# Four tiles instead of two in the product with w_out1, z in six half-pair places, and a new opening list

## The chip, the cores and the metric

The kernel runs on one NeuronCore of a Trainium2 chip. What counts is the device time of one execution in microseconds (us), and lower is better. Five engines work side by side, each through its own instructions in order: TensorE (PE, matrix products; its weight loads are listed as PEld), VectorE (DVE), ScalarE (ACT), GpSimd (POOL) and SyncE (SP), which here only issues DMAs. An engine waits on semaphores of the others.

## The reference, cut to what matters

```python
# attention in chunks of 64 keys: 8 batches, 8 heads, 576 tokens, head size 64
scores = scale * q_c @ k_c.T;  attn = softmax(scores);  out = attn @ v_c
x = out.transpose(0, 2, 1, 3).reshape(4608, 512)
# first layer, 512 -> 1024 -> 512
h = x @ w_in1
solu = h * softmax(h)
z = (solu - mean(solu)) / sqrt(var(solu) + 1e-6)
y = (z * g_ln) @ w_out1
# second layer, 512 -> 2048 -> 512
h = y @ w_in2
out = (max(h, 0) + alpha * min(h, 0)) @ w_out2
```

Inputs of the layers are 64-bit floats in DRAM. Their words are turned into float32 on the chip.

## The kernel before, in words

The 4608 tokens are 36 tiles of 128. **The first part** runs them through attention, the first layer's two products and the normalisation between. Beside that it converts all weights: a unit is one 128x512 piece of a weight matrix; units 0 to 7 are w_in1, 8 to 15 w_out1, 16 to 47 the second layer's, which are also split into a high and a low half and written back to DRAM. **The second part** computes the second layer with a scheme of seven products in place of eight, for the rows w_in2 first and w_out2 after it.

Each float32 product is three products of halves (function `mm3`): high by high, high by low, low by high. The halves of x are `xh` and `xl`, those of z `zh` and `zl`, those of the weights `wi_h`, `wi_l`, `wo_h`, `wo_l`.

The steps of a tile i in the order of its data have short names, which the lists use:

- attention: `q`, `v` loads; `qk` scores (PE, 32 products); `qm` maximum and difference (DVE), `qe` exponential (ACT), `qs` sum and reciprocal (DVE), `qn` scaling (POOL for the first twelve tiles, then DVE); `tr` transposition (PE), `te` its copy (ACT), `pv` product with v (PE); `xh` (ACT) and `xl` (DVE) the halves of x.
- first layer: `hm` x by w_in1 (PE, 24 products of 512 columns), `hx` maximum (DVE), `he` exponential (ACT), `so` product of h and softmax (DVE), `sq` squares (ACT), `zv`, `pw`, `zs` variance and scaling (DVE, POOL, DVE), `zt` transposition (PE, 8), `zh` (ACT) and `zl` (DVE) its halves; `ya`, `yb` two blocks of z by w_out1 (PE), `ye` copy of the result from PSUM (ACT) and its store to DRAM.
- weights, unit u: `f` load, `p` two sign parts (ACT, two instructions), `s` or `S` their difference (POOL or DVE), `l` low word (DVE, two instructions), `a` or `A` sum (POOL or DVE), `h` high half (ACT), `o` or `O` low half (POOL or DVE).

The order is written by hand. `FIRST` is the list of all steps up to tile 10, `STEP` the steps of one iteration i of the loop over the other tiles (`ya-5` is the step `ya` of number i-5), `CONV` the weight steps inside it, `LAST` the end of the first part, in which `sy` are steps of the second part. Every engine takes its own instructions in this order.

Before, a group of the product with w_out1 is two tiles (YT = 2, 256 columns), and its 512 output rows are four blocks of 128 rows. Step number s computes two of the blocks for the group s // 2, in `ya` and `yb`: 24 products of 256 columns each (8 pieces of the inner size 1024 times 3 halves). z has three buffers of two tiles, zh and zl apart. The first group can start once tile 1 is through. In the opening the words of w_in1 (`rawt`) lie in these z buffers, and so do the halves of x of tiles 2 to 5 (`xt`). The result goes from PSUM with one ACT copy for two blocks and a DMA on ACT's queue. `ps_a` has three PSUM banks, which `sc` (scores), `et` (transposed) and `xd` (attention output) take in turn; the result of `hm` has two banks, that of `zt` two, that of `ya` and `yb` one.

At the start of the second part the weights `w` of its eight blocks are loaded on SP's queue: the first two into room left by x, the next ones into room that z, w_out1 and the result of the product leave.

Of the kernel before, what the change touches and what calls it, by code (L numbers as in the profile page):

```python
# [42 lines left out]
def order(text):  # L43
# [12 lines left out]
    xl4 p9 te5 a8 qk7 qn6 pv5 hx0 he0 qm7 f11 s9 q9 p10 tr6 so0 l9 qe7 qs7 v8 qk8 s10 sq0 zv0 hm1
    xh5 pw0 h8 q10 qk9 qm8 a9 l10 p11 zs0 v6 te6 xl5 o8 qe8 a10 h9 hx1 he1 qs8 zt0 so1 f12 qm9 zh0
    qn7 tr7 p12 zl0 sq1 f13 s11 q11 s12 pv6 q12 zv1 h10 f14 qe9 l11 hm2 p13 pw1 v9 zs1 te7 f15 a11
    qs9 hx2 qn8 h11 l12 zt1 he2 o10 pv7 xh6 tr8 so2 xl6 p14 hm3 al0 S14 a12 qn9 te8 zh1 o11 zl1 xh7
    o9 qk10 sq2 zv2 l14 tr9 pw2 zs2 xl7 S13 zt2 p15 hx3 l13 h12 a14 he3 s15 so3 f16 te9 zh2 pv8 zl2  # L60
    pv9 h14 hm4 qm10 a13 h13 f18 f17 v12 o12 O13 p16 o14 sq3 l15 zv3 qe10 A15 pw3 zs3 f20 p18 v10
    f19 qs10 s16 zt3 h15 o15 l16 v11 hx4 s18 he4 p17 so4 A16 sq4 f21 s17 ya0 yb0 zv4 hm5 p20 ye0 zh3
    l17 ya1 yb1 pw4 l18 hm6 hx5 f22 he5 p19 qn10 a17 ye1 zs4 zl3 so5 a18 p21 xh8 sq5 S19 zv5 zt4 pw5
    h18 zs5 ya2 yb2 zh4 hx6 he6 h17 o18 zt5 zl4 l19 zh5 so6 o17 sq6 zv6 pw6 zl5 hm7 s20 zs6 zt6 ye2
    h16 hx7 he7 so7 xh9 xl8 zh6 sq7 ya3 yb3 zv7 S21 l20 pw7 zs7 hm8 tr10 zl6 hx8 zt7 qk11 a19 te10
    pv10 xl9 he8 f23 so8 sq8 zh7 hm9 qm11 zv8 ye3 zl7 xh10 hx9 ya4 yb4 pw8 qe11 zs8 he9 so9 sq9 h19
    zv9 qs11 qn11 A20 pw9 xl10 zs9 zt8 o16
# [5 lines left out]
    ya-5 conv+1 xh+1 xl+1 zv+0 pw+0 qs+2 zs+0 qn+2 yb-5  # L73
# [16 lines left out]
def tile_chunk_attention_solu_prelu(  # L90
# [74 lines left out]
    def phase1():  # L165
        with ExitStack() as c1, ExitStack() as c0:
# [11 lines left out]
            ztp = R("zt", YL // 2)  # L178
# [21 lines left out]
            wo_h = wop.tile([128, KF1, DM], F32R, name="wo_h")  # L200
            wo_l = wop.tile([128, KF1, DM], F32R, name="wo_l")
# [6 lines left out]
            for kk in range(KF1):  # L208
                units.append((w_out1[kk * 128:(kk + 1) * 128, :], wo_h[:, kk], wo_l[:, kk]))
# [89 lines left out]
            def run_post(k):  # L299
# [14 lines left out]
            xt = [ztp.tile([128, 2, 2, NP, 128], F32R, name=f"xe{k}", tag=t) for k, t in enumerate(("zh", "zl"))]  # L314
# [92 lines left out]
            def pv(i):  # L407
# [3 lines left out]
                ps = ps_a.tile([128, NP, 2, CH], F32, name="xd", tag="a")  # L411
# [80 lines left out]
            def zscale(i):  # L492
                st, s = ss.pop((i, 5))
                nc.vector.tensor_scalar(
                    out=s, in0=s, scalar1=st[:, 4:5], scalar2=st[:, 7:8], op0=ALU.add, op1=ALU.mult
                )
                zz[i] = s

            ztt, zps = {}, {}

            def ztr(i):
                z = zz.pop(i)
                ps = ps_z.tile([128, KF1, 128], F32, name="zt", tag="zt")
# [23 lines left out]
            ypools = [ps_y]  # L527

            def ymm(s, m):
                j, half = divmod(s, 2)  # L530
                assert ("zl", 2 * j + 1) in done and all(("o", u) in done for u in range(UI, UO))
                zh, zl = ztt[j]
                if m == 0:
                    ypend[s] = ypools[(s + 1) % len(ypools)].tile([128, 2, YG], F32, name="yps", tag="yps")
                else:
                    assert ("ya", s) in done
                ps = ypend[s][:, m]
                c = slice((2 * half + m) * 128, (2 * half + m + 1) * 128)
                for kk in range(KF1):
                    mm3(ps, wo_h[:, kk, c], wo_l[:, kk, c], zh[:, kk], zl[:, kk], kk == 0, kk == KF1 - 1)  # L540
                if half and m:
                    del ztt[j]

            def yevac(s):
                assert ("yb", s) in done
                j, half = divmod(s, 2)
                y = yp.tile([128, 2, YG], F32, name="ysb", tag="ysb")
                nc.scalar.activation(out=y, in_=ypend.pop(s), func=AF.Copy)  # L548
                g, o = divmod(j * YG, 2 * SG)
                nc.scalar.dma_start(out=y_dram[g][:, 2 * half:2 * half + 2, o:o + YG], in_=y)  # L550
# [13 lines left out]
                zt=ztr, zh=zhigh, zl=zlow, ya=lambda s: ymm(s, 0), yb=lambda s: ymm(s, 1), ye=yevac,  # L564
# [4 lines left out]
                {k: TILES for k in "q v qk qm qe qs qn tr te pv xh xl hm hx he so sq zv pw zs zt zh zl ya yb ye".split()},  # L569
# [43 lines left out]
            with tc.tile_pool(name="ps_y2", bufs=1, side="left", space=PSUM, reuse_waits="tile") as ps_y2:  # L613
                ypools.append(ps_y2)
                for name, i in LAST:
                    if name == "sy":
                        next(second)
                    else:
                        emit(name, i)
# [477 lines left out]
```

## Time and profile before

| | us |
|---|---|
| median of three runs | 1294.31 (1292.63 to 1296.69) |
| the profiled execution | 1296.48 |
| its span in the trace | 1294.1 |
| PE busy in the span | 1246.7 (96%) |
| DVE, ACT, POOL busy | 947.8, 686.5, 328.2 |
| products with w_out1, of 128x256 | 3 x 576 |

The trace gives times from the span's start. Matmuls are pipelined and their listed durations overlap; the pace of a stream is read from start to start. The granted clock of TensorE (PEclk) is given as a share of its full speed. The stretches of the opening are cut where `hx0`, `hm5` and `hm10` begin.

### The profile page before, as it was taken

How to read it: one execution, taken by the hardware profiler on the slowest of the kernel's cores; microseconds unless marked ns; L12 is line 12 of the kernel's file. 1: busy time of each engine (PE TensorE's matmuls, PEld its weight loads, DVE VectorE, ACT ScalarE, POOL GpSimd, SP SyncE). 2: the span in 40 equal slices, each digit the busy share in tenths (PEclk: the TensorE clock that was granted, in tenths of full speed). 3: DMA queues.
4: the chain of work that ended last, by engine and by line, in shares of the span. 5: the costliest groups of instructions: out<-in, count | busy, mean ns of one | idle time of the engine just before them, and what ended most of it. 6: DMA issues, size and time to landing. Idle time of an engine off the chain costs nothing.

```text
span 1294.1 us, 23429 instructions
## 1 busy us (share of the span) xinstructions
PE 1246.7 (96%) x9024; PEld 1152.0 (89%) x9024; DVE 947.8 (73%) x1423; ACT 686.5 (53%) x1140; POOL 328.2 (25%) x309
## 2 busy tenths in 40 slices
PE   4789899999999989999999999999999999999998
PEld 4678789999889989899999999999999788888898
DVE  6996677777878766535878787877876959768684
ACT  5685355555556555434757575766634434444443
POOL 4563245343657464332020202020000000000000
PEclk8799999999999999999999999999999999999999
DMA  8443246564656463269642434436996647375462
GB/s 304 161 132 108 80 149 187 162 188 154 201 192 221 155 212 106 75 244 339 225 153 110 159 111 159 149 121 247 365 344 192 236 138 266 120 246 172 147 227 98
DMA packets 144655, 237.99 MB, mean 184 GB/s; under 512 B 13856, under 2 KB 99360, under 8 KB 142496
## 3 DMA queue, kind: packets, MB, share of 16 engines
q1 hardware_dynamic: 134592, 226.27, 51.1%
q10 hardware_dynamic: 9792, 9.44, 2.1%
q8 instruction: 71, 1.16, 0.4%
q0 software_dynamic: 160, 0.79, 0.1%
q14 instruction: 40, 0.33, 0.1%
HBM read 149.68 MB, written 86.77 MB: 183 GB/s over the span
## 4 chain that ended last, share of the span: by engine, by line
PE 48%; DMA 2%; DVE 1%; ACT 0%; issue 0%; DVEq 0%; ACTq 0%; SPq 0%
PE oz L955 7%; PE ov L955 7%; PE hz L722 7%; PE ox L955 7%; PE hx L722 7%; PE hv L722 7%; PE oy L955 3%; PE hy L722 3%; DMA gd<-g 2%; DMA rc<-gd 1%; DVE rt L636 0%; DVE rb L636 0%; DVE rlo L636 0%; ACT rhi L639 0%; ACT g L639 0%
## 5 line engine op out<-in xcount | busy, mean ns | idle before, releaser
L161 PE MATMUL yps<-zh,wo_h 128*128 128x256 f32 x576 | 165.4, 287 | 0.7 <-ACT ysb L548 0.7
L163 PE MATMUL yps<-zh,wo_l 128*128 128x256 f32 x576 | 163.0, 283 | 0.0
L162 PE MATMUL yps<-zl,wo_h 128*128 128x256 f32 x576 | 162.9, 283 | 0.0
L761 DVE SCALAR_TENSOR_TENSOR g<-ng,nal,g 128x384 f32<-128x384 f32 x192 | 124.7, 649 | 50.4 <-ACT g L639 50.3
L639 ACT ACTIVATE ng<-g 128x384 f32<-128x384 f32 x144 | 75.8, 526 | 117.2 <-DVE g L633 117.2
L722 PE MATMUL hv<-th,w 128*128 128x384 f32 x384 | 113.0, 334 | 0.3 <-DVE g L633 0.3
L722 PE MATMUL hz<-th,w 128*128 128x384 f32 x384 | 113.1, 335 | 0.2 <-DVE wv L633 0.2
L722 PE MATMUL hx<-th,w 128*128 128x384 f32 x384 | 113.0, 334 | 0.0
L161 PEld LDWEIGHTS yps<-zh,wo_h 128*128 128x128 f32 x576 | 110.5, 192 | 1.0 <-ACT ysb L548 0.9
L162 PEld LDWEIGHTS yps<-zl,wo_h 128*128 128x128 f32 x576 | 110.4, 192 | 0.1
L163 PEld LDWEIGHTS yps<-zh,wo_l 128*128 128x128 f32 x576 | 110.3, 192 | 0.0
L955 PE MATMUL oz<-rhi,w 128*128 128x512 f32 (+1 forms) x304 | 93.8, 369 | 0.8 <-DVE osb L633 0.8
L955 PE MATMUL ox<-rhi,w 128*128 128x512 f32 (+1 forms) x304 | 93.7, 369 | 0.0
L955 PE MATMUL ov<-rhi,w 128*128 128x512 f32 (+1 forms) x304 | 93.7, 369 | 0.0
L636 POOL TENSOR_TENSOR yt<-y,y 128x384 f32<-128x384 f32 x24 | 27.1, 1152 | 234.2 <-DMA y<-yd 136.8
L639 ACT ACTIVATE rhi<-rt 128x1024 fp32r<-128x1024 f32 (+1 forms) x56 | 54.5, 984 | 59.5 <-DVE rt L636 16.3
L443 PE MATMUL h<-wi_h,xh 128*128 128x512 f32 x256 | 71.0, 399 | 6.5 <-DVE sl L471 4.6
L639 ACT ACTIVATE g<-g 128x384 f32<-128x384 f32 x144 | 75.2, 522 | 3.1
L523 DVE TENSOR_TENSOR zl<-zt,zh 128x1024 fp32r<-128x1024 f32 x36 | 44.0, 1221 | 43.5 <-ACT zh L518 43.5
L636 DVE TENSOR_TENSOR rlo<-rt,rhi 128x1024 fp32r<-128x1024 f32 (+1 forms) x56 | 62.3, 1125 | 13.8 <-ACT rhi L639 13.7
L722 PEld LDWEIGHTS hz<-th,w 128*128 128x128 f32 x384 | 70.7, 188 | 0.7 <-DVE wv L633 0.7
L722 PEld LDWEIGHTS hv<-th,w 128*128 128x128 f32 x384 | 70.7, 188 | 0.6 <-DVE g L633 0.6
(176 smaller groups left out, 3320.6 us busy)
## 6 DMA issues: line engine op xcount, KB each, us to landing
gd<-g SPq DMA_DIRECT2D x192, 192.0 KB, 1.8
qkt<-in_qk SPq DMA_DIRECT2D x36, 512.0 KB, 5.7
w<-wid SPq DMA_DIRECT2D x8, 1792.0 KB, 9.6
w<-wod SPq DMA_DIRECT2D x8, 1792.0 KB, 9.6
rc<-gd SPq DMA_DIRECT2D x24, 512.0 KB, 4.3
rd<-gd SPq DMA_DIRECT2D x24, 512.0 KB, 5.1
raw<-in_moe_w_out SPq DMA_DIRECT2D x24, 511.8 KB, 4.2
vt<-in_v SPq DMA_DIRECT2D x36, 256.0 KB, 5.2
```

The source lines that it names most:

```text
L161: nc.tensor.matmul(o, lh, rh, start=first, stop=False)
L162: nc.tensor.matmul(o, lh, rl, start=False, stop=False)
L163: nc.tensor.matmul(o, ll, rh, start=False, stop=last)
L443: nc.tensor.matmul(ps[:, n], xh[:, kk], w[:, kk, 512 * n:512 * n + 512], start=(kk == 0 and w is wi_h), stop=False,)
L523: nc.vector.tensor_tensor(out=zl, in0=ps, in1=zh.bitcast(F32), op=ALU.subtract)
L636: eng.tensor_tensor(out=out, in0=a, in1=b, op=ALU.subtract)
L639: nc.scalar.activation(out=out, in_=in_, func=func, **k)
L722: nc.tensor.matmul(self.ps[x], w[:, a, i, k], d[:, k], start=(p not in CHAINED and k + j == 0), stop=(k == 1 and j == 2), skip_group_check ...
L761: nc.vector.scalar_tensor_tensor(out=self.g[t], in0=self.n[t], scalar=nal_sb[:, f:f + 1], in1=self.g[t], op0=ALU.mult, op1=ALU.add)
L955: nc.tensor.matmul(bank[key, m][:, :n], W[2 * j + k][:, a, i, 128 * m:128 * m + 128], d[:, k], start=(p not in CHAINED and j + k + q == 0) ...
```

## The change

The product takes groups of four tiles (YT = 4): 512 columns in one matmul, 12 products in a `ya` and 12 in a `yb`. z lies in one tile `zz` of six places. A place holds both halves of half of the inner size (4 of 8 pieces) for a pair of tiles (256 columns); a table `Z_SLOTS` says which two places a pair takes. The matmul's moving operand is thus two runs of 256 columns, from two places. In a group, steps 0 and 1 compute a block each, and steps 2 and 3 together two blocks, the first half of the inner size for both in step 2 (`ya`, `yb`), the second half in step 3. A group's first pair of places is free for new z after step 2, the second after step 3.

`ye` stores one block of 512 columns, not two of 256, by two DMAs on SP's queue; a new step `yx` does so for the block that is complete after `ya` of step 3. PSUM: the result has two banks, `sc` and `et` one each, and `xd` shares et's bank (in the first eight tiles that of the result). w_in1's words lie in the room of `wo_h` and `wo_l`, which are made when unit 8 is converted. `FIRST` is a new order; `STEP` gets `yx-5` at its end; `LAST` is adapted, without the additional PSUM pool.

```diff
-YT = 2
+YT = 4
 YG = 128 * YT
-YL = 6
+YP = 256
...
 STEP = order(
     """
     q+3 v+3 ye-6 zh-2 zl-2 conv+0 hm+0 tr+1 te+1 qk+2 hx+0 he+0 qm+2 qe+2 pv+1 zt-1 so+0 sq+0
-    ya-5 conv+1 xh+1 xl+1 zv+0 pw+0 qs+2 zs+0 qn+2 yb-5
+    ya-5 conv+1 xh+1 xl+1 zv+0 pw+0 qs+2 zs+0 qn+2 yb-5 yx-5
...
-    zh34 zl34 ye30 ya31 yb31 zt35 zh35 zl35 ye31 ya32 yb32 sy0 sy1 ye32 ya33 yb33 sy2 sy3
-    ye33 ya34 yb34 sy4 sy5 ye34 ya35 yb35 sy6 sy7 ye35
+    zh34 zl34 ye30 ya31 zt35 yb31 zh35 zl35 yx31 ye31 ya32 yb32 sy0 sy1 ye32 ya33 yb33 sy2 sy3
+    ye33 ya34 yb34 sy4 sy5 ya35 yb35 sy6 yx35 sy7 ye35
...
+Z_SLOTS = (
+    ((0, 1), (2, 4)), ((3, 5), (0, 2)), ((1, 4), (0, 3)), ((2, 5), (0, 1)), ((3, 4), (0, 2)),
+    ((1, 5), (0, 3)), ((2, 4), (0, 1)), ((3, 5), (0, 2)), ((1, 4), (0, 3)),
+)
...
-            ps_a = L("ps_a", 3, space=PSUM)
+            ps_a = L("ps_a", 1, space=PSUM)
...
-            ps_y = R("ps_y", 1, space=PSUM)
+            ps_y = R("ps_y", 2, space=PSUM)
...
+            zz = ztp.tile([128, 6, 2, KF1 // 2, YP], F32R, name="zz")
             rawt = [
-                ztp.tile([128, 2, 512, 4], U16, name=f"wraw{kk}", tag="zh" if kk % 2 == 0 else "zl")
-                for kk in range(K1)
+                r[:, k] for t in ("h", "l")
+                for r in [wop.tile([128, 2, 2, 512, 4], U16, name=f"wraw{t}", tag=f"wo_{t}")] for k in range(2)
             ]
...
+            def yblock(j, m, h):
+                a, b = sorted(x[h] for x in Z_SLOTS[j])
+                if h == 0:
+                    ypend[j, m] = ps_y.tile([128, YG], F32, name="yps", tag="yps")
+                ps = ypend[j, m]
+                zh, zl = (zz[:, a:b + 1:b - a, n] for n in range(2))
+                c = slice(m * 128, m * 128 + 128)
+                for k in range(KF1 // 2):
+                    kk = KF1 // 2 * h + k
+                    mm3(ps, wo["h"][:, kk, c], wo["l"][:, kk, c], zh[:, :, k], zl[:, :, k], kk == 0, kk == KF1 - 1)
+
+            def ymm(s, n):
+                j, q = divmod(s, YT)
+                assert ("zl", YT * j + 3) in done and all(("o", u) in done for u in range(UI, UO))
+                assert n == 0 or ("ya", s) in done
+                if q < 2:
+                    yblock(j, q, n)
                 else:
+                    yblock(j, 2 + n, q - 2)
+
+            def ystore(j, m):
+                y = yp.tile([128, YG], F32, name="ysb", tag="ysb")
+                nc.scalar.activation(out=y, in_=ypend.pop((j, m)), func=AF.Copy)
+                pairs = (0, 1) if Z_SLOTS[j][0][0] < Z_SLOTS[j][1][0] else (1, 0)
+                for c, p in enumerate(pairs):
+                    g, o = divmod(j * YG + p * YP, 2 * SG)
+                    nc.sync.dma_start(out=y_dram[g][:, m, o:o + YP], in_=y[:, c * YP:(c + 1) * YP])
```

The opening list is new as a whole. It moves steps on every engine; three places are shown.

**ACT at the very start.** `pos` and `neg` are step `p` of a unit, `e` is `qe0`, `ets` is `te0`. Before:

```order
L555 ACTIVATE mhalf<-mhalf 128x1
L139 ACTIVATE pos<-wraw_133,b_64 128x512
L140 ACTIVATE neg<-wraw_133,b_64 128x512
L139 ACTIVATE pos<-wraw_133,b_64 128x512
L140 ACTIVATE neg<-wraw_133,b_64 128x512
L381 ACTIVATE e<-e 128x512
L139 ACTIVATE pos<-wraw_134,b_64 128x512
```

Now, at the same place:

```order
L585 ACTIVATE mhalf<-mhalf 128x1
L142 ACTIVATE pos<-wrawh,b_64 128x512
L143 ACTIVATE neg<-wrawh,b_64 128x512
L391 ACTIVATE e<-e 128x512
L142 ACTIVATE pos<-wrawh,b_64 128x512
L143 ACTIVATE neg<-wrawh,b_64 128x512
L414 ACTIVATE ets<-et 128x512
```

The first exponential now stands behind one unit's `p` and not behind two.

**PE in the opening, around its first product with w_out1.** `zt` is the transposition of z of tile 3 in both, `h` is `hm`. Before, `hm4` ends here, `zt3` follows, then the first `ya`:

```order
L443 MATMUL h<-wi_h,xe_138 128x512 x4
L443 MATMUL h<-wi_l,xe_138 128x512 x4
L449 MATMUL h<-wi_h,xe_138 128x512 x8
L505 MATMUL zt<-ident,sl 128x128 x8
L161 MATMUL yps<-zh,wo_h 128x256
L162 MATMUL yps<-zl,wo_h 128x256
L163 MATMUL yps<-zh,wo_l 128x256
```

Now `hm5` stands between the transposition and the first `ya` (which is number 1), and each product has 512 columns:

```order
L518 MATMUL zt<-ident,sl 128x128 x8
L456 MATMUL h<-wi_h,zz 128x512 x4
L456 MATMUL h<-wi_l,zz 128x512 x4
L456 MATMUL h<-wi_h,zz 128x512 x4
L456 MATMUL h<-wi_l,zz 128x512 x4
L462 MATMUL h<-wi_h,zz 128x512 x8
L164 MATMUL yps<-zz,wo_h 128x512
L165 MATMUL yps<-zz,wo_h 128x512
L166 MATMUL yps<-zz,wo_l 128x512
```

`ya0` and `yb0`, which stood ahead of `hm5`, now come after it and after `ya1`, `yb1` and `hm6`.

**SP at the start of the second part.** `w20` to `w24` are the weights of its blocks 0 to 4, `y11` to `y21` its first inputs, `yd` the first part's result in DRAM. Before (the stores of that result are on ACT's queue):

```order
L684 DMA y21_6848<-yd0_65 128x2x384
L658 DMA w20_6850<-wid_71 128x3584
L658 DMA w21_6852<-wid_71 128x3584
L658 DMA w22_7209<-wid_71 128x3584
L658 DMA w23_7211<-wid_71 128x3584
L658 DMA w24_7233<-wid_71 128x3584
```

Now:

```order
L712 DMA y21_6098<-yd0_65 128x2x384
L686 DMA w20_6100<-wid_71 128x3584
L686 DMA w21_6102<-wid_71 128x3584
L569 DMA yd5_70<-ysb_6141 128x256
L569 DMA yd4_69<-ysb_6141 128x256
L569 DMA yd5_70<-ysb_6145 128x256
L569 DMA yd4_69<-ysb_6145 128x256
L569 DMA yd5_70<-ysb_6188 128x256 x2
L569 DMA yd5_70<-ysb_6225 128x256 x2
L569 DMA yd5_70<-ysb_6289 128x256 x2
L569 DMA yd5_70<-ysb_6297 128x256 x2
L686 DMA w22_6338<-wid_71 128x3584
```

Twelve stores of the first part stand between `w21` and `w22`.

## Rows read from the trace of the kernel before

**Rows 1.** The page's first part: busy time, share, instructions of each engine

```profile
PE 1246.7 (96%) x9024; PEld 1152.0 (89%) x9024; DVE 947.8 (73%) x1423; ACT 686.5 (53%) x1140; POOL 328.2 (25%) x309
```

**Rows 2.** Stretches of the opening: window, length, busy us per engine, PEclk, DMA share

```profile
10.80:45.15 34.35, 22.33 (x373) 19.72 (x373) 31.79 (x53) 20.31 (x35) 18.59 (x16) 0.75 0.75 270
...
55.75:109.25 53.50, 46.35 (x485) 38.99 (x483) 47.98 (x85) 41.31 (x67) 30.65 (x27) 0.97 0.46 147
109.25:173.07 63.82, 59.57 (x420) 53.41 (x421) 37.71 (x63) 28.87 (x46) 17.91 (x17) 0.97 0.24 75
173.07:533.73 360.66, 355.78 (x3556) 324.27 (x3554) 268.15 (x444) 198.22 (x321) 186.94 (x173) 1.00 0.54 176
```

**Rows 3.** One iteration of the loop, PE: start us, us, instruction, count

```profile
271.21 0.36 PE L161 MATMUL yps<-zh,wo_h 128*128 128x256 f32 x1
271.41 0.28 PE L162 MATMUL yps<-zl,wo_h 128*128 128x256 f32 x1
...
277.05 1.09 PE L443 MATMUL h<-wi_h,xh 128*128 128x512 f32 x4
...
282.52 0.60 PE L399 MATMUL et<-ident,e 128*128 128x128 f32 x4
...
285.91 0.36 PE L161 MATMUL yps<-zh,wo_h 128*128 128x256 f32 x1
```

**Rows 4.** Stretches of the second part, one product form each: 384, 512 columns

```profile
700.00:750.00 50.00, 50.00 (x290) 50.00 (x289) 38.83 (x68) 31.49 (x68) 9.44 (x8) 1.00 0.40 143
...
1100.00:1150.00 50.00, 50.00 (x223) 41.40 (x222) 32.72 (x31) 21.43 (x22) 0.00 (x0) 1.00 0.45 149
```

**Rows 5.** The opening, PE, in order of time

```profile
102.42 0.36 PE L161 MATMUL yps<-zh,wo_h 128*128 128x256 f32 x1
...
109.25 1.17 PE L443 MATMUL h<-wi_h,xe 128*128 128x512 f32 x4 [0.84 <-DVE sl L471]
...
137.12 2.06 PE L443 MATMUL h<-wi_h,xh 128*128 128x512 f32 x4 [3.23 <-DVE sl L471]
138.97 1.83 PE L443 MATMUL h<-wi_l,xh 128*128 128x512 f32 x4
140.64 1.09 PE L443 MATMUL h<-wi_h,xh 128*128 128x512 f32 x4
...
160.91 1.21 PE L443 MATMUL h<-wi_h,xh 128*128 128x512 f32 x4 [1.03 <-DVE sl L471]
```

**Rows 6.** The first steps, ACT

```profile
7.59 0.73 ACT L140 ACTIVATE neg<-wraw,b 128x512 uint16<-128x512 uint16 x1
...
10.16 0.61 ACT L381 ACTIVATE e<-e 128x512 f32<-128x512 f32 x1
```

**Rows 7.** DVE ahead of hm5: step qs10, then hx4 and so4

```profile
101.37 0.67 DVE L385 TENSOR_REDUCE r<-e 128x8 f32<-128x512 f32 x1
...
103.20 1.08 DVE L151 TENSOR_SCALAR g<-a 128x512 uint16<-128x512 uint16 x1
...
104.93 1.22 DVE L457 TENSOR_REDUCE st<-h 128x1 f32<-128x1024 f32 x1
...
107.81 1.28 DVE L471 SCALAR_TENSOR_TENSOR sl<-h,st,eh 128x1024 f32<-128x1024 f32 x1
```

**Rows 8.** An iteration of the loop on DVE, ACT and SP

```profile
289.29 0.69 DVE L434 TENSOR_TENSOR xl<-xd,xh 128x512 fp32r<-128x512 f32 x1 [1.85 <-ACT xh L429]
...
291.95 0.60 ACT L548 ACTIVATE ysb<-yps 128x512 f32<-128x512 f32 x1 [2.69 <-PE yps L163]
...
294.56 0.38 SPq L232 DMA_DIRECT2D wid<-hi  x1
```

**Rows 9.** Loads of the second part's weights, SP, and their landing; its first product

```profile
579.55 0.80 SPq L658 DMA_DIRECT2D w<-wid  x2
...
DMA to landing us min/median/max: 8.2/9.2/13.3
...
590.95 0.34 PE L722 MATMUL hx<-th,w 128*128 128x384 f32 x1
```

More of the change, by code (lines that the diff above doesn't have):

```diff
@@ L56 @@
[L56 to L65, printed above, removed]
@@ L66 @@
-    pv10 xl9 he8 f23 so8 sq8 zh7 hm9 qm11 zv8 ye3 zl7 xh10 hx9 ya4 yb4 pw8 qe11 zs8 he9 so9 sq9 h19
-    zv9 qs11 qn11 A20 pw9 xl10 zs9 zt8 o16
+    q0 f0 p0 q1 qk0 f1 q8 qk1 qm0 f3 qe0 q9 f2 p1 qs0 s0 qn0 tr0 te0 l0 v0 a0 q2 pv0 q12 qm1 f5 p3 q7 S1
+    qe1 qk2 l1 q3 A1 f4 v1 qs1 p2 S2 h1 qm2 xh0 q4 v2 l2 h0 p5 qe2 s3 xl0 v4 qk3 qn1 o0 qs2 O1 a2 f8 p4
+    qm3 qn2 l3 tr1 v7 f7 f6 te1 h2 tr2 q5 qe3 pv1 a3 S4 v3 f10 xh1 qs3 qk4 o2 qn3 te2 p7 qm4 qe4 pv2 S5
+    l4 h16 tr3 l5 A4 xh2 q6 qs4 te3 a5 p6 s7 xl2 f9 xl1 qk5 qm5 p8 h4 v8 v5 h5 qn4 h3 s6 O4 tr4 f11 qe5
@@ new lines @@
+    l13 xl6 f21 a13 te8 h12 f17 zt2 he3 zh2 f19 p16 f20 tr9 so3 h13 zl2 sq3 qm10 hm4 s15 pv8 qk11 te9
+    l15 s16 xh7 zv3 h14 A15 p18 pw3 s18 o16 O13 o14 l16 h15 o9 hx4 o12 he4 zs3 o15 zt3 so4 sq4 zh3 l18
+    zv4 qe10 p17 zl3 A16 hm5 s17 hx5 ya1 he5 l17 yb1 so5 sq5 ye1 hm6 p19 a17 ya0 qs10 zv5 pw4 h18 xl7
+    zs4 xh8 pw5 f22 hx6 zt4 zh4 he6 yb0 zs5 a18 zt5 zl4 h19 ya2 xl8 hm7 p20 so6 S19 zh5 s20 ye0 v9 sq6
+    zl5 zv6 pw6 pv9 zs6 hx7 he7 so7 p21 sq7 zt6 yb2 zh6 hm8 v12 v10 xh9 h17 zv7 xl9 l19 o18 hx8 pw7 zl6
@@ L68 @@
+    qn10 tr10 a19 zs7 qm11 o17 te10 he8 ya3 yb3 zt7 so8 pv10 sq8 zh7 zl7 hm9 l20 f23 ya4 zv8 hx9 S21 ye3
+    he9 pw8 ye2 yx3 xh10 A20 zs8 so9 sq9 qe11 zv9 qs11 pw9 xl10 qn11 zs9 yb4 zt8
     """
@@ L208, in phase1 @@
             for kk in range(KF1):
-                units.append((w_out1[kk * 128:(kk + 1) * 128, :], wo_h[:, kk], wo_l[:, kk]))
+                units.append((w_out1[kk * 128:(kk + 1) * 128, :], None, None))
             UI, UO = 2 * K1, 2 * K1 + KF1
@@ L345, in unit_hi @@
                 else:
-                    his[u] = units[u][1]
+                    if u == UI:
+                        assert all(("l", x) in done for x in range(UI))
+                        for t in "hl":
+                            wo[t] = wop.tile([128, KF1, DM], F32R, name=f"wo_{t}", tag=f"wo_{t}")
+                    his[u] = wo["h"][:, u - UI]
                     nc.scalar.activation(out=f, in_=f, func=AF.Copy, scale=g_sb[:, u - UI:u - UI + 1])
@@ L396, in tr @@
                 e = ee.pop((i, 1)).rearrange("q (j w) k -> q j (w k)", w=2)
-                ps = ps_a.tile([128, NP, 128], F32, name="et", tag="a")
+                ps = ps_a.tile([128, NP, 128], F32, name="et", tag="et")
                 for p in range(NP):
@@ L410, in pv @@
                 v = vs.pop(i)
-                ps = ps_a.tile([128, NP, 2, CH], F32, name="xd", tag="a")
+                if i < 8:
+                    ps = ps_y.tile([128, NP, 2, CH], F32, name="xd", tag="yps")
+                else:
+                    ps = ps_a.tile([128, NP, 2, CH], F32, name="xd", tag="et")
                 for c in range(2):
@@ L526, in phase1 @@
             ypend = {}
[L527 to L534, printed above, removed]
-                else:
[L536 to L542, printed above, removed]
+            def yblock(j, m, h):
[8 more added lines that the diff above has]
+                    mm3(ps, wo["h"][:, kk, c], wo["l"][:, kk, c], zh[:, :, k], zl[:, :, k], kk == 0, kk == KF1 - 1)
@@ L544, in yevac, with yfirst @@
             def yevac(s):
                 assert ("yb", s) in done
[L546 to L550, printed above, removed]
+                j, q = divmod(s, YT)
+                if q != 2:
+                    ystore(j, q)
+            def yfirst(s):
+                j, q = divmod(s, YT)
+                if q == 3:
+                    ystore(j, 2)
@@ L612, in phase1 @@
             next(second)
[L613 to L619, printed above, removed]
+            for name, i in LAST:
+                if name == "sy":
+                    next(second)
+                else:
+                    emit(name, i)
         next(second, None)
```

61 lines of the change are left out of this document (32 added, 29 removed).

## The prediction

> **What bounds the kernel now.** I read the page's first part first: PE is busy for 1246.7 of 1294.1 us [rows 1], so 47 us are all that waiting costs it, and a saving has to come from PE's own work or from those waits. The stretches tell where they lie. From 173.07 on PE is the bound: in 360.66 us of the loop it is idle for 4.9, at full clock, and DVE, the next busiest, has 268.15 [rows 2]. The opening is different. From 10.80 to 45.15 DVE is busy for 31.79 of 34.35 us, and from 55.75 to 109.25 for 47.98 of 53.50, while PE has gaps and a granted clock of 0.75 and 0.97 [rows 2]. So up to `hm5` (109.25) DVE sets the pace, from there PE does, with two waits for DVE left [rows 5]. I price the loop in PE's products and the opening in DVE's steps.
>
> **The products.** One iteration of the loop lasts 285.91 - 271.21 = 14.70 us on PE. Its 48 narrow products take 277.05 - 271.21 = 5.84: the first 0.20, the other 47 take 5.64, 120 ns each [rows 3]. Right behind stand the 24 products of `hm`, 512 columns wide, in 282.52 - 277.05 = 5.47, 228 ns each [rows 3]. Two other widths fit: 290 products of 384 columns in 50 us are 172 ns each, 223 of 512 are 224 [rows 4]. So a product costs about 0.41 ns per column and 12 to 16 ns besides, and that second part is paid once in place of twice. After the change a tile has 24 products of 512 columns. I take `hm`'s pace and the 0.08 us that the first product after a transposition costs more today: 5.47 + 0.08 = 5.55. That saves 0.29 us a tile, 10.4 over 36.
>
> No row shows a moving operand of two runs, as z is now. Its bounds: one run's price, 224 ns, or that of two products, 240, where nothing is saved. I take 228, since the number of columns is what the price follows in all three widths.
>
> The Trainium skill ("TensorE: Matmul & The Clock Gate", section "Back-to-back issue gap") speaks against this change: it gives a warm gap of N/2.4 + 2.5 ns, so that a merged pair would save 2.5 ns, 2.2 us over 864 pairs. The trace doesn't agree: 120 and 228 ns stand where the formula gives 109 and 216, and the measured rows decide.
>
> **What the opening loses.** Before, `ya0` and `yb0` (102.42 to about 108.3) run while PE would only wait for `so4` [rows 5]. Now the first group needs tile 3's z, so these products come after `hm5`, where PE is the bound. From `hm5` to `hm10` PE needed 63.82 us. In them are waits of 3.23 and 1.03 for `so6` and `so8` and, after the first, eight products at half pace: 140.64 - 137.12 = 3.52 us in place of 1.82, 1.7 lost [rows 5]. That leaves 57.9 of work. Now five tiles' products with w_out1 lie there and not four: 5 x 5.55 = 27.7 against 4 x 5.84 = 23.4, so 62.3. (`qk11` leaves the stretch and `pv9` enters it, about alike.)
>
> **What it may gain.** Two things. First, `hm5` comes earlier. The first exponential ends up behind one pair of sign parts and not two: ACT's `neg` started at 7.59 and the exponential at 10.16 [rows 6]; right behind that `neg` it would start at about 8.3, 1.9 us earlier, and DVE's chain starts with its result. Two steps, `xl7` and `qs10`, now stand behind `so4` on DVE: 103.20 - 101.37 = 1.83 for `qs10` [rows 7], some 0.6 to 0.7 for `xl7` (0.69 for its like [rows 8]). All other steps of DVE up to `so4` are the same in another order. Against it: the load of `q1` is issued ahead of unit 1's words on SP, which can hold `p1` back; and ACT, POOL and DVE wait for each other at other places. These bounds are 0 and the sum of both parts, 4.3, with the idle time of DVE in rows 2 (2.56 + 5.52) to be won or lost on top. I take 3.7: `hm5` at 105.6.
>
> Second, the two waits. A tile's chain from `hx` to the next `hm` is 109.25 - 104.93 = 4.3 us [rows 5, 7]. PE now has between `hm6` and `hm7` `ya0`, `yb0`, `ya2` and two transpositions (10 us), between `hm8` and `hm9` `ya3`, `yb3` and more (8). Both cover the chain. The tight places are ahead of `hm6` (5.55 against 4.3 and a weight step on DVE in between) and ahead of `hm8` (one block and `pv9`). I put 1.0 there. Ahead of `hm5` PE now has nothing but `pv8`, `qk11` and `zt3` and waits some 3 us for `so4`; after such a wait eight products ran at half pace, so 1.8 more. In all 2.8 against 6.0 now.
>
> **Steps that cost nothing, and their cover.** The stores leave ACT's queue for SP's, 72 of half the size for 36. On SP a store waits for ACT's copy, and behind it stand the writes of converted weights, the next words and loads. In the loop the copy starts at 291.95 and SP's next entry is issued at 294.56, waiting for ACT's later work [rows 8], so the store fits ahead of it; loads run three tiles ahead. `zh` of a group's third tile needs the places that the last `yb` read, which is what `ye`, ahead of it on ACT, waits for anyway. `et` and `xd` share a bank, so `tr` waits for the previous `xl`: that starts at 289.29 [rows 8], `tr` comes at 282.52 + 14.70 = 297.2 [rows 3]. `ya` of a new group needs the `zl` of the same iteration, which has `hm`'s 5.47 us ahead of it. `yx` needs ACT once in four tiles, and ACT is half idle [rows 1].
>
> At the start of the second part `w22` and `w23` were issued at 579.55, 11.4 us ahead of the first product at 590.95 [rows 9]. Now z is one tile and twelve stores stand ahead of them, the last of which needs the last product: they are issued some 2 us after the first product, 13 later than now. They land in 8.2 to 13.3 us [rows 9]. The third block needs `w22` after two blocks of 42 products of 172 ns [rows 4], 14.5 us. So 10.2 to 15.3 against 14.5: hidden, or up to 0.8. I take 0.
>
> **The sum.** `hm10` at 109.25 - 3.7 + 62.3 + 2.8 = 170.65 against 173.07: 2.4 earlier. The 31 tiles' products left save 31 x 0.29 = 9.0. Together 11.4: the profiled execution from 1296.48 to 1285.1 (span 1282.7), and, since it stands 2.2 above the median of 1294.31, the median to **1282.9 us**.
>
> **Rivals.** (a) *The wide product is no cheaper than two narrow ones* (240 ns), because of the two runs, or because the fixed part isn't what merging saves. Then `hm10` comes at 109.25 - 3.7 + 63.7 + 2.8 = 172.1, 1.0 earlier, and nothing follows: 1293.3. For it: no row shows such an operand. Against it: three widths on one line. The skill's formula belongs here; by it the time would be 2.2 lower, 1291.1. (b) *The opening gains nothing*: `hm5` at 109.25 as before, and 6.0 us of waits and half pace move elsewhere: 109.25 + 62.3 + 6.0 = 177.6, 4.5 later, less 9.0: 1289.8. For it: DVE is near full up to there, and its list is only another order of nearly the same steps. (c) *Slower: PE stays at the lower clock up to `hm5`*, since its only other work there, `ya0` and `yb0`, is gone and it waits for each `so`. At that level 24 products take 10.6 us and not 5.47; with 4.3 of chain that is 14.9 per tile against (104.93 - 55.75) / 4 = 12.3 now [rows 2, 7]: 4 x 2.6, and 5.1 for `hm5`, in all 15.5, so 1298.4. It decides from three quarters of these blocks at half pace, where the 11.4 are gone. Against it: a granted clock of 0.97 in that stretch, with gaps there already [rows 2].
>
> **How the numbers follow.** Chances: the forecast 0.66, (a) 0.08, (b) 0.20, (c) 0.06. The forecast's own range is 1276.5 (`hm5` four us earlier, fewer waits) to 1288. To hold 8 in 10 the range takes in most of (b): 1276.5 to 1291.5. About 0.3% (3.9 us) is what a measurement here can tell from no change. Faster than 1290.4: nearly all of the forecast and over half of (b), 0.76; within: (a), the rest of (b), 0.18; slower: (c), 0.06.
>
> **What would show it.** In the profile after: narrow products gone, starts of the wide ones 224 to 230 ns apart (240 says (a)); an iteration of 14.4 us; `hm5` near 105.6 and `hm10` near 170.7; no wait for `so6`; the third block's first product without a wait for SP. `hm5` later than 109 or a clock under 0.9 from 55 to 105 would say (b) or (c). Wrong altogether would be a new wait in the loop, for `zl` ahead of `ya` or for SP.

## The result, and the profile after

The changed kernel takes **1279.16 us** (median of 4 runs, 1278.49 to 1281.57) against 1295.07 (1292.63 to 1296.69) for the kernel before in the same comparison: a ratio of 0.9882, 95% interval 0.9861 to 0.9903, so 15.9 us less. The forecast was 1282.9 with a range of 1276.5 to 1291.5, and a chance of 0.76 for "faster". The time is inside the range; the balance below shows that it got there by large errors of opposite sign, so by luck.

The page of the changed kernel, first part (span; busy time, share and instructions of each engine), beside [rows 1]:

```profile
span 1279.7 us, 21741 instructions
PE 1236.0 (97%) x8160; PEld 1108.6 (87%) x8160; DVE 933.9 (73%) x1423; ACT 682.4 (53%) x1140; POOL 326.6 (26%) x309
```

PE has 864 products fewer and is busy for 10.7 us less. Its idle time went from 47.4 us to 43.7. The profiled execution took 1281.57 us, 2.4 above the median.

One iteration on PE, as in [rows 3] (start us, duration us, instruction, count):

```profile
202.97 0.39 PE L166 MATMUL yps<-zz,wo_l 128*128 128x512 f32 x1
203.20 1.07 PE L456 MATMUL h<-wi_h,xh 128*128 128x512 f32 x4
...
212.04 0.48 PE L164 MATMUL yps<-zz,wo_h 128*128 128x512 f32 x1
212.35 0.39 PE L165 MATMUL yps<-zz,wo_h 128*128 128x512 f32 x1
...
217.14 0.39 PE L165 MATMUL yps<-zz,wo_h 128*128 128x512 f32 x1
217.37 0.39 PE L166 MATMUL yps<-zz,wo_l 128*128 128x512 f32 x1
217.59 0.62 PE L456 MATMUL h<-wi_h,xh 128*128 128x512 f32 x2
```

The wide products start 0.22 to 0.23 us apart, the first of a tile, behind a transposition, 0.31; a tile's 24 take 217.59 - 212.04 = 5.55 us. From one `hm` to the next are 217.59 - 203.20 = 14.39 us, against 14.70 before.

The opening on PE, as in [rows 5]: `hm4` behind a wait, `hm5` at 97.94, the first and the last product of the first `ya` and `yb` behind it, `hm6`, and `hm10`:

```profile
85.20 2.05 PE L456 MATMUL h<-wi_h,zz 128*128 128x512 f32 x4 [3.21 <-DVE sl L484]
...
97.94 1.16 PE L456 MATMUL h<-wi_h,zz 128*128 128x512 f32 x4 [1.14 <-DVE sl L484]
...
103.49 0.39 PE L164 MATMUL yps<-zz,wo_h 128*128 128x512 f32 x1
...
108.70 0.39 PE L166 MATMUL yps<-zz,wo_l 128*128 128x512 f32 x1
...
108.93 1.07 PE L456 MATMUL h<-wi_h,xh 128*128 128x512 f32 x4
...
159.91 1.17 PE L456 MATMUL h<-wi_h,xh 128*128 128x512 f32 x4
```

Here, with no transposition right ahead of them, a tile's 24 wide products take 108.93 - 103.49 = 5.44 us. The waits for `so6` and `so8` that [rows 5] show are gone. The stretches, as in [rows 2] (window, length, busy us and instructions of PE, PEld, DVE, ACT, POOL, granted clock, DMA share, GB/s):

```profile
10.80:44.01 33.21, 21.84 (x344) 19.75 (x345) 29.24 (x55) 21.79 (x38) 17.39 (x16) 0.90 0.74 279
54.53:97.94 43.41, 37.85 (x366) 31.28 (x365) 37.88 (x74) 35.29 (x57) 29.04 (x26) 0.92 0.48 146
97.94:159.91 61.97, 61.97 (x349) 51.55 (x349) 35.75 (x67) 30.29 (x50) 19.77 (x20) 1.00 0.37 110
159.91:520.00 360.09, 355.03 (x3027) 299.40 (x3027) 269.58 (x446) 198.32 (x326) 188.89 (x177) 1.00 0.53 175
```

From `hx0` to `hm5` DVE has 37.88 us of work where it had 47.98, and from `hm5` to `hm10` PE never waits.

The start of the second part, as in [rows 9]. Its first product starts at 567.26. SP's queue from there (issue us, us, DMA, count):

```profile
569.05 1.29 SPq L686 DMA_DIRECT2D w<-wid  x3
574.07 1.32 SPq L794 DMA_DIRECT2D gd<-g  x2
575.43 2.03 SPq L712 DMA_DIRECT2D y<-yd  x4
581.67 6.00 SPq L794 DMA_DIRECT2D gd<-g  x2
```

The landing of the stores issued from 573 to 582 us, and of the weight loads issued from 566 to 600 us (17.4 is that of the third, issued at 569.91):

```profile
DMA to landing us min/median/max: 11.2/13.2/13.7
...
DMA to landing us min/median/max: 6.9/11.7/17.4
```

And the rows of DVE, ACT and PE in order of time, with the idle time ahead of each and what ended it:

```profile
587.85 0.56 DVE L661 TENSOR_TENSOR g<-hz,u 128x384 f32<-128x384 f32 x1 [6.60 <-DMA gd<-g]
...
589.87 0.47 ACT L667 ACTIVATE s<-hx 128x384 f32<-128x384 f32 x1
...
590.39 0.69 PE L750 MATMUL hx<-th,w 128*128 128x384 f32 x1 [4.22 <-ACT s L667]
```

Read from the last row back: PE waits 4.22 us for ACT's copy, ACT stands behind steps that wait for DVE, DVE waits 6.60 us for a free `g` (six buffers), and a `g` is free when its store has landed. The first stores landed 11.2 to 13.7 us after their issue. At the same place the kernel before had 2.3 to 9.1 us and one wait of DVE, 1.1 us:

```profile
DMA to landing us min/median/max: 2.3/6.5/9.1
```

The first store, issued at 574.07, landed at 587.76, 0.5 us behind the third weight load (587.27).

The balance of the two profiled executions:

| from, to | before | after | difference |
|---|---|---|---|
| start to `hm5` | 109.25 | 97.94 | -11.3 |
| `hm5` to `hm10` | 63.82 | 61.97 | -1.9 |
| `hm10` to the second part's first product | 417.9 | 407.4 | -10.5 |
| from there to the end | 703.1 | 712.4 | +9.3 |
| span | 1294.1 | 1279.7 | -14.4 |

The open questions were thus: is the -10.5 the width of the products, what gave 11.3 where 3.7 was forecast, and what took 9.3 back.

### The profile page after: what moved, and what is told of

It is laid out like the page before. It is cut to its first block, busy times and chain, and to the rows that moved or that the text cites. A ratio compares the mean times of both kernels' runs of the same rounds, so it can differ in the third digit from the quotient of the medians.

```text
span 1279.7 us, 21741 instructions
## 1 busy us (share of the span) xinstructions
PE 1236.0 (97%) x8160; PEld 1108.6 (87%) x8160; DVE 933.9 (73%) x1423; ACT 682.4 (53%) x1140; POOL 326.6 (26%) x309
## 5 line engine op out<-in xcount | busy, mean ns | idle before, releaser
L164 PE MATMUL yps<-zz,wo_h 128*128 128x512 f32 x288 | 115.2, 400 | 0.0
L166 PE MATMUL yps<-zz,wo_l 128*128 128x512 f32 x288 | 112.4, 390 | 0.0
L165 PE MATMUL yps<-zz,wo_h 128*128 128x512 f32 x288 | 112.2, 390 | 0.0
L750 PEld LDWEIGHTS hx<-th,w 128*128 128x128 f32 x384 | 71.3, 189 | 5.8 <-ACT s L667 5.8
L456 PE MATMUL h<-wi_l,xh 128*128 128x512 f32 x256 | 68.8, 390 | 0.2 <-POOL wi_l L362 0.2
L492 ACT ACTIVATE eh<-sl,st 128x1024 f32<-128x1024 f32 x36 | 41.5, 1152 | 45.0 <-DVE st L487 45.0
L750 PE MATMUL hx<-y,w 128*128 128x384 f32 x192 | 64.5, 336 | 0.0
```

The source lines that it names most:

```text
L164: nc.tensor.matmul(o, lh, rh, start=first, stop=False)
L165: nc.tensor.matmul(o, lh, rl, start=False, stop=False)
L166: nc.tensor.matmul(o, ll, rh, start=False, stop=last)
L456: nc.tensor.matmul(ps[:, n], xh[:, kk], w[:, kk, 512 * n:512 * n + 512], start=(kk == 0 and w is wi_h), stop=False,)
L492: nc.scalar.activation(out=e, in_=s, func=AF.Square, bias=st[:, 4:5], accum_out=st[:, 5:6])
L750: nc.tensor.matmul(self.ps[x], w[:, a, i, k], d[:, k], start=(p not in CHAINED and k + j == 0), stop=(k == 1 and j == 2), skip_group_check ...
```

## The experiments

### The width alone

> The changed kernel with each product with w_out1 split again into two of 256 columns, everything else in the new order and places. Theory (the width is what the loop gains by): starts 118 to 122 ns apart, 5.7 to 5.9 us for a tile's 48 in place of 5.44, an iteration 0.3 us longer, and over 36 tiles 9 to 12 us: 1288 to 1291 us. Rival (the loop's gain is from the order and the groups of four tiles): under 3 us, at most 1282.

```diff
-                for k in range(KF1 // 2):
-                    kk = KF1 // 2 * h + k
-                    mm3(ps, wo["h"][:, kk, c], wo["l"][:, kk, c], zh[:, :, k], zl[:, :, k], ...)
+                for r in range(2):
+                    o = ps[:, r * YP:(r + 1) * YP]
+                    for k in range(KF1 // 2):
+                        # the same three products, moving operand zh[:, r, k] or zl[:, r, k]
```

In this kernel two sums are open in one bank at a time, and its y isn't the reference's; its products are twice as many and half as wide, and the steps' order is the changed kernel's. It took 1288.70 us (ratio to before 0.996, 0.9949 to 0.9971), 9.5 more than the changed kernel. Two successive products and the next `hm`:

```profile
217.68 0.28 PE L557 MATMUL yps<-zz,wo_h 128*128 128x256 f32 x1
217.80 0.28 PE L558 MATMUL yps<-zz,wo_l 128*128 128x256 f32 x1
217.92 1.09 PE L456 MATMUL h<-wi_h,xh 128*128 128x512 f32 x4
```

They start 0.12 us apart and the iteration is back at 14.70 (217.92 - 203.22). In everything else the kernel is the changed one, so the rival (order and groups) falls: the width is worth 0.31 us a tile, 24 x (2 x 0.120 - 0.227).

### The loads at the start of the second part

> The changed kernel, but at the start of the second part one load of w_in2's blocks is issued ahead of the first product's block and one more per block after it, in place of two ahead and a third right behind them. Theory (the first results' stores to DRAM lie in the DMA queues behind 5.5 MB of weights and the tiles that they free are missed 14 us later): the stores land in under 8 us, DVE's wait of 6.60 us and PE's of 4.22 go, and with them the products at half pace: 5 to 9 us less, 1270 to 1274. Rival (the third block waits for its own weights, which are issued as late as before): the wait stays within 2 us of 4.2, and the time within 0.3% of 1279.

```diff
-            for b in range(NL, NL + 2):
+            for b in range(NL, NL + 1):
                 load_w(b, wi_dram)
...
-                        if s == 0 and k == 1 and NL + 2 + b < NB2:
-                            load_w(NL + 2 + b, wi_dram)
+                        if s == 0 and k == 1 and NL + 1 + b < NB2:
+                            load_w(NL + 1 + b, wi_dram)
```

> The opposite: three loads of w_in2's blocks are issued at once and a fourth right behind them. Theory (stores behind weights): 1.8 MB more ahead of the stores at about 400 GB/s, 4.6 us, so a wait of PE near 8.8 us in place of 4.2 and 1282 to 1286. Rival (the third block's own weights): its load is the first of the three as before, so nothing changes: within 0.3% of 1279.

The same two places with `NL + 3`. Measured: one load, **1272.65** us (0.9839, 0.9821 to 0.9858), 6.5 less than the changed kernel; more loads, 1282.78 (0.991, 0.9892 to 0.9928), 3.6 more. Two views follow for each kernel: PE's waits at the start of the second part (tile and line <- whom: us in total, times, longest), and the first 40 us from the first product as a stretch, for before and after the next 32 too; for the two new kernels also the landing of the first two stores. Before, with only one wait, of 0.2 us:

```profile
591.00:631.00 40.00, 39.85 (x228) 39.12 (x228) 26.24 (x46) 22.26 (x49) 8.79 (x8) 1.00 0.91 325
631.00:663.00 32.00, 32.00 (x187) 32.00 (x186) 26.07 (x46) 21.61 (x45) 0.00 (x0) 1.00 0.37 129
```

After:

```profile
PE hx L750 <- ACT s L667: 5.1, 2, 4.2
```

```profile
567.30:607.30 40.00, 34.59 (x181) 33.63 (x180) 19.41 (x35) 16.60 (x36) 8.10 (x8) 0.91 0.94 362
607.30:639.30 32.00, 32.00 (x187) 32.00 (x186) 26.97 (x48) 22.42 (x46) 0.00 (x0) 1.00 0.39 142
```

One load at a time:

```profile
PE hx L750 <- ACT s L667: 2.1, 1, 2.1
```

```profile
DMA to landing us min/median/max: 7.2/7.5/7.8
...
565.90:605.90 40.00, 37.94 (x210) 37.62 (x209) 23.70 (x41) 20.03 (x43) 8.12 (x8) 0.96 0.97 362
```

More loads at once:

```profile
PE hx L750 <- ACT s L667: 10.8, 2, 8.8
```

```profile
DMA to landing us min/median/max: 17.7/18.0/18.2
...
565.10:605.10 40.00, 29.18 (x157) 28.22 (x155) 16.05 (x29) 13.44 (x29) 8.11 (x8) 0.91 0.95 374
```

The wait follows the bytes ahead of the stores: 2.1, 4.2 and 8.8 us, the last as forecast, while the third block's own load was the first in line in all three. The first two stores landed 7.2 to 7.8, 13.2 to 13.7 and 17.7 to 18.2 us after their issue, the first of them each time 0.5 us behind the last weight load issued ahead of it. The rival falls. (From the third store on there is a second way in which the loads hold up the stores: in the changed kernel SP's next issues waited 5.9 us in all for a weight load to land. The long waits of DVE are for the first stores.) What a wait costs is best read from the products done: 228 + 187 = 415 in 72 us before, 181 + 187 = 368 after. The 47 that are missing are 8.1 us at 172 ns [rows 4], most of the 9.3 given back; of the rest, 0.9 lies in the part with w_out2. One load at a time is 19 short.

### The stores put first

> As the kernel with one load per block, but the loads of the fourth to the eighth block of w_in2 start one block later still (the fourth in the second block, and so on), so that only one load, 1.8 MB, lies ahead of the first results' stores. Theory (stores behind weights): DVE's waits for the stores, 4.1 us with one load per block, go below 1.5, PE's 2.1 below 0.5, and 1.5 to 3 us are won on 1272.65: 1269.5 to 1271. Rival (the loads are then too late): the fourth or a later block waits for its weights by over 1 us, and the time is 1273 or more.

```diff
-            for b in range(NL, NL + 2):
+            for b in range(NL, NL + 1):
...
-                        if s == 0 and k == 1 and NL + 2 + b < NB2:
-                            load_w(NL + 2 + b, wi_dram)
+                        if s == 0 and k == 1 and NL < NL + b < NB2:
+                            load_w(NL + b, wi_dram)
```

> The changed kernel with the loads at the start of the second part put behind the stores that they held up: one load of w_in2 ahead of the first block as in the two kernels before, the fourth block's right behind the first block's two first stores (8 us earlier on SP than where the fourth block missed it by 1.3 us), one more at the same place of each later block, and the next group's y at the end of the second block in place of its start. Theory (stores behind weights): no wait of PE over 0.5 us up to 40 us after the first product, no half pace, 701 to 704 us from the first product to the end of the span, and 1269 to 1271.5 us. Rival (the sum of the transfers is what counts, in any order): one of the waits comes back at over 1 us, and the time stays at 1272 to 1274.

```diff
+                        if s == 0 and k == 5 and NL + 1 + b < NB2:
+                            load_w(NL + 1 + b, wi_dram)
...
-                            if (b, k) == (1, 0):
+                            if (b, k) == (1, 4):
                                 load_y(s + 1)
```

Measured: 1271.57 (0.9825, 0.9807 to 0.9842) and 1271.73 (0.9828, 0.9813 to 0.9842), both within the interval of the kernel with one load at a time. The forecasts were 1269.5 to 1271 and 1269 to 1271.5, so both times lie just above them and below the rivals' (from 1273 and from 1272). In the first, PE's wait for the stores' tiles went (DVE's is still 2.2 us, where under 1.5 was expected), and the rival's wait came in its place; in the second neither is left, with the same transfers in another order, so the rival of the second falls. PE's wait and the first 40 us of the first:

```profile
PE hx L750 <- DMA w<-wid: 1.3, 1, 1.3
```

```profile
564.80:604.80 40.00, 38.72 (x223) 38.36 (x223) 25.33 (x45) 21.47 (x47) 8.79 (x8) 1.00 0.91 340
```

and of the second:

```profile
PE hz L750 <- DVE wv L661: 0.3, 1, 0.3
```

```profile
565.20:605.20 40.00, 39.67 (x227) 39.06 (x227) 25.66 (x45) 21.79 (x47) 9.02 (x8) 1.00 0.93 352
```

227 products in 40 us are those of before (228). So the mechanism can be removed in full. The last 3 us that the trace promises over one load at a time (17 products) hardly show in the medians, which are 0.9 apart. In the second, 704.7 us from the first product to the end are just above the 701 to 704 expected; the last part alone, behind the last product with w_in2, took between 351.8 and 354.2 us in the profiles of this section and the next two, so a difference of 2 us there tells nothing.

### The stores of y on ACT's queue

> The changed kernel with the 72 stores of y back on ACT's queue. The prediction's step (they cost nothing on SP's queue in the loop): within 0.3% of 1279. At the start of the second part the loads of the third and fourth block no longer stand behind twelve stores on SP, but they still wait for the last product with w_out1, so the wait of PE stays within 1 us of 4.2. Rival (SP's queue is what delays those loads): they are issued over 3 us earlier and 3 us or more are won.

```diff
-                nc.sync.dma_start(out=y_dram[g][:, m, o:o + YP], in_=y[:, c * YP:(c + 1) * YP])
+                nc.scalar.dma_start(out=y_dram[g][:, m, o:o + YP], in_=y[:, c * YP:(c + 1) * YP])
```

> The same, and the 72 stores of y back on ACT's queue. If what the stores on ACT gained alone (1276.23 against 1279.16) came from the start of the second part, nothing is left of it here: within 0.1% of the kernel beside it. If it came from the loop or the opening, it is 2 to 3 us faster than that: 1266 to 1269.

1276.23 (0.9861, 0.9846 to 0.9876) alone, 2.9 less than the changed kernel and inside the 0.3% of the prediction's step; **1269.25** (0.9806, 0.9792 to 0.9819) together with the order of loads above, 2.5 less than that order alone and just above the 1266 to 1269 expected. In the first kernel PE's longest wait at the start of the second part is 3.8 us, within 1 us of 4.2, and the loads come only 1.5 us earlier after the first product (0.2 us behind it in place of 1.8), so the rival falls. The gain is there twice. In the second comparison it isn't from the start of the second part, where nothing was left to win: 1.9 of the 2.6 us between the two profiles lie between `hm10` and the second part's first product, 405.5 us here and 407.3 to 407.4 in the six profiles of the changed kernel's order with the stores on SP's queue. In the first kernel that stretch is 406.5, 0.8 less, and 1.6 more are won from there to the last product with w_in2. Why the stores' queue matters stays open: the plain iterations of the loop are 14.39 us in all of these kernels. (One iteration behind one that converts two units took 18.12 us in the last kernel's profile and 19.6 to 19.7 in the others', that with the stores alone on ACT among them.) This last kernel is 9.9 us faster than the changed one and 25.5 faster than the one before.

### The first exponential on ACT

> The changed kernel with one step moved back: the first tile's exponential behind the second pair of sign parts on ACT, as it stood before the change. The prediction's step (1.9 us of hm5's lead come from there): hm5 at 99.5 to 100.2 in place of 97.94, and 1280.5 to 1281.5 us. Rival (what counts is which steps of DVE run beside one of POOL, and any shift of the start deals those anew): the number of lengthened DVE steps up to hm5 leaves 9 to 13, and hm5 moves by more than 3 us or not at all.

```diff
-    q0 f0 p0 q1 qk0 f1 q8 qk1 qm0 f3 qe0 q9 f2 p1 qs0 s0
+    q0 f0 p0 q1 qk0 f1 q8 qk1 qm0 f3 q9 f2 p1 qe0 qs0 s0
```

> The kernel before with that one step moved forward: the first tile's exponential ahead of the second pair of sign parts on ACT. The prediction's step: hm5 1.9 us earlier, at 107.3, and 1.9 us off the time, 1292.2 to 1293. Rival (which DVE steps run beside POOL's): hm5 moves by more than 4 us or not at all, with the number of lengthened DVE steps away from 23.

```diff
-    q0 f0 p0 f1 p1 qk0 q1 s0 f2 qm0 qe0 qs0
+    q0 f0 p0 f1 qk0 qm0 qe0 p1 q1 s0 f2 qs0
```

Measured: 1281.92 (0.9905, 0.9892 to 0.9919), 2.8 more than the changed kernel, with `hm5` at 99.49 and 12 lengthened DVE steps; and 1293.12 against 1294.10 (0.9994, 0.9984 to 1.0004), with `hm5` at 104.92 and 23 of them. The counts didn't move, so a shift of the start alone doesn't deal out anew which steps run beside POOL: that rival falls by the counts, though the 4.3 us by which `hm5` came earlier in the second are as much as it asked for. In the first the exponential starts at 10.89 and not at 10.16 as before the change, since the second unit's words arrive later there, so its 2.8 us (a little over the 1280.5 to 1281.5 expected) are for 2.65 us of delay and not for 1.9. The price of the step is between -0.5 and 2.1 by the second: 1.9 fits both, but the second can't be told from nothing. The 4.3 us of `hm5` in the second are mostly the difference of the two executions that were profiled: 1291.31 is 1.8 under that kernel's median, 1296.48 is 2.2 over that of before.

### POOL's steps beside DVE's

Every step of DVE up to `hm5` that took over 0.15 us more than the shortest of its kind stood beside one of POOL's. Two of before, each as POOL's row and DVE's, which ends 0.14 to 0.15 us behind POOL's:

```profile
13.82 1.20 POOL L336 TENSOR_TENSOR f<-f,a 128x512 f32<-128x512 f32 x1 [0.69 <-DVE f L154]
...
14.04 1.13 DVE L151 TENSOR_SCALAR g<-a 128x512 uint16<-128x512 uint16 x1
...
44.71 1.46 POOL L145 TENSOR_TENSOR a<-pos,neg 128x512 bf16<-128x512 bf16 x1 [1.45 <-DVE f L336]
...
45.06 1.25 DVE L151 TENSOR_SCALAR g<-a 128x512 uint16<-128x512 uint16 x1
```

and two of after, the first beside POOL, the second alone:

```profile
17.92 1.27 POOL L362 TENSOR_TENSOR wi_l<-f,wi_h 128x512 fp32r<-128x512 f32 x1
...
18.30 1.04 DVE L154 TENSOR_SCALAR g<-a 128x512 uint16<-128x512 uint16 x1
...
23.61 0.28 DVE L154 TENSOR_SCALAR g<-a 128x512 uint16<-128x512 uint16 x1
```

Alone this step takes 0.24 to 0.29 us. Counted so, 23 steps before lost 17.0 us beside POOL, and 11 after lost 7.7: a difference of 9.3. (In the seven other profiles with this opening it is 11 to 13 steps and 7.3 to 9.4 us.) Not every step beside one of POOL's is longer: of DVE's reductions 18 before and 22 after overlapped one, and none was. In the groups up to `hm5` (line, engine, operation, tiles, count | busy us, mean ns | idle), before and then after:

```profile
L151 DVE TENSOR_SCALAR g<-a 128x512 uint16<-128x512 uint16 x17 | 11.5, 678 | 0.8 <-POOL a L145 0.6
```

```profile
L154 DVE TENSOR_SCALAR g<-a 128x512 uint16<-128x512 uint16 x18 | 6.7, 372 | 0.1
```

To see whether POOL is the cause, two kinds of its steps in the opening were made short:

> The kernel before with two kinds of POOL's steps cut in the opening to a few columns: the normalisation of the first twelve tiles' exponentials (8 of 512 columns) and the addition to the converted parts of w_in1 and w_out1 (2 of 512), so that weights and attention are not the reference's; names and order of all steps stay. 8 of the 23 lengthened DVE steps up to hm5 met one of these two kinds, 4.8 of 17.0 us. Theory (DVE waits while POOL runs): these lengthenings go, the rest stays about as it is: 10 to 13 us, and hm5 is 4 to 8 us earlier. Rival (these DVE steps are long by themselves, by their data or the transfers): still 20 or more lengthened steps and 15 us or more.

```diff
-                eng.tensor_tensor(out=parts[u], in0=parts[u], in1=tops.pop(u), op=ALU.add)
+                c = slice(0, 2) if eng is nc.gpsimd and u < UO else slice(0, 512)
+                eng.tensor_tensor(out=parts[u][:, c], in0=parts[u][:, c], in1=tops.pop(u)[:, c], op=ALU.add)
...
+                if i < 12:
+                    nc.gpsimd.tensor_tensor(out=e[:, :, 0:1], in0=e[:, :, 0:1], in1=r.unsqueeze(2), op=ALU.mult)
```

13 lengthened steps and 10.0 us in place of 23 and 17.0, and `hm5` at 101.27, 8.0 earlier; 1287.67 us (0.9955, 0.9942 to 0.9969). The same step of DVE, now:

```profile
L151 DVE TENSOR_SCALAR g<-a 128x512 uint16<-128x512 uint16 x17 | 8.7, 514 | 0.1
```

The DVE steps themselves weren't touched, so the length that went was POOL's doing; the rival falls. The 6.4 us of the median aren't all that, since PE's waits for the exponentials that POOL scales also shrank, from 11.4 us to 7.7.

## Why the prediction was right or wrong, step by step

- **The products: right.** 5.55 us per tile was forecast; 5.55 was measured in the loop and 5.44 in the opening, where `hm` and no transposition stands ahead. The starts are 0.227 apart, so two runs in the moving operand cost nothing. The first product behind a transposition does cost 0.08 more. The iteration is 14.39 for 14.4. The formula that the prediction took from the Trainium skill ("TensorE: Matmul & The Clock Gate", section "Back-to-back issue gap"), where it is given for an isolated product, would have let the merging save 2.2 us in all; undoing it cost 9.5, so the measurement decides against it for this stream.
- **The loop: right, a little small.** 10.5 for 9.0: 31 x 0.31 = 9.6, and 0.9 besides, nearly all of it in the first iteration behind `hm10` (15.67 us before, 14.51 after), where two halts of PE, of 0.3 and 0.4 us, are gone.
- **`hm5` to `hm10`: work right, waits wrong.** The 62.3 of work were 61.97. The 2.8 (1.0 of waits at the tight places and 1.8 of half pace behind a wait for `so4`) never came: `so6` to `so9` were all there in time, and ahead of `hm5` PE waited 1.14 us and not 3. The products at half pace behind a long wait stand at `hm4` instead (14 products at half pace behind the wait of 3.21 shown above).
- **`hm5`: the step that failed low.** 105.6 was forecast, 97.94 came (95.5 to 96.5 in the seven other profiles with this opening). The prediction counted DVE's steps and said that they "are the same in another order". They are, but not of the same length: the new order puts fewer of them beside a step of POOL, 9.3 us less. The term that was mis-sized is DVE's work up to `so4`, which the prediction priced as a fixed sum; DVE's busy time up to `hm5` fell from 90.5 us to 80.4, and its idle time by 1.2. The rows had a sign of it: the step of 1.08 us in [rows 7] takes 0.24 to 0.29 alone. Both parts that it did name are in the trace: the exponential starts at 8.24 in place of 10.16 [rows 6], and DVE has four steps fewer ahead of `hm5`.
- **The start of the second part: the step that failed high.** The term "hidden, or up to 0.8. I take 0" stands against 9.3. The issue time was right (569.05, 1.8 us after the first product), and so was the third block's own weight, which came in time. What the prediction didn't ask is who stands behind these loads: the first results' stores in the DMA queues, and behind them `g`'s buffers, DVE, ACT and PE.
- **The stores on SP's queue:** within 0.3%, as said, but not nothing: 2.5 to 2.9 us in two comparisons.
- **The rivals.** (a) falls by the pace, 227 and not 240. (b) and (c) fall by `hm5`; the clock did fall behind `hm4`'s wait, but the stretch up to `hm5` has 0.92.

In sum -11.3 - 1.9 - 10.5 + 9.3 = -14.4 where -3.7 + 1.3 - 9.0 + 0 = -11.4 was forecast: the gain was underrated by 7.6 + 3.2 + 1.5 = 12.3 and the loss of 9.3 wasn't seen, which leaves the 3.0 by which the total was off. So close a total is luck; the mechanism is right for the products and the loop; in the opening and at the start of the second part what decided wasn't in the sum.

## What to carry to other kernels

When a load is moved later, ask what it will stand in front of, not only who waits for it: a store that frees a buffer can hold up three engines. When an order is changed where DVE and POOL both work, DVE's time isn't a constant; compare the shortest and the mean duration of one kind of step, and see which POOL step stands beside the long ones. And merging two narrow products into a wide one is worth its fixed part, 13 ns each here, where PE is the bound.

## What the runs showed of the hardware that was not expected

**DVE beside POOL.** Each lengthened step ends 0.03 to 0.55 us behind one of POOL's. A step of 128x8 that takes 0.17 us alone took up to 1.07, and one of 128x512 in 16 bits up to 1.25 in place of 0.28. The Trainium skill ("SBUF — State Buffer", section "SBUF: two separate sides") says that the two share a pair of ports, which some of DVE's steps need (those in a mode with two ports, or with two inputs in SBUF), by "an exclusive lock, not a bandwidth split", held for a whole instruction. The trace agrees, in that the lengthened steps end with POOL's and the reductions keep their length, and adds the price: up to `hm5` 17.0 us, where DVE was busy for 90.5.

**The clock behind a wait.** PE's 4.22 us of idle time at the start of the second part cost more than themselves (stretches of after, as above):

```profile
585.20:590.39 5.19, 0.97 (x6) 0.65 (x5) 2.19 (x5) 1.91 (x5) 0.00 (x0) 0.88 1.10 411
590.39:594.00 3.61, 3.61 (x11) 3.61 (x12) 2.09 (x4) 0.73 (x2) 2.51 (x3) 0.50 1.05 445
594.00:597.00 3.00, 3.00 (x13) 3.00 (x13) 1.06 (x1) 1.43 (x4) 3.00 (x4) 0.66 1.03 398
```

At a granted clock of 0.50, the lower of the two levels, PE did 11 products in 3.61 us and then 13 in 3.00, where 38 fit at full clock: 14 x 0.172 = 2.4 us more. With one load at a time the wait of 2.1 us left the first 40 us at 0.96, with the wait of 1.3 us at 1.00.
